# Where a helper's instructions stand in the queues: attention behind the last MLP tile, weight conversion behind the last but one

## The chip, the cores and the metric

One core of a Trainium2 chip runs the whole program. The metric is device microseconds from the first to the last instruction plus what lies around them, as measured by the runs. TensorE (PE), VectorE (DVE), ScalarE (ACT), GpSimd (POOL) and SyncE (SP, which here only issues transfers) each work off their own queue in order.

## What is computed

```python
scores  = scale * x @ state.T ;  a  = softmax(scores)  ; xread = a @ state      # 8 batches, 8 heads, x 512x64
scores2 = scale * state @ x.T ;  a2 = softmax(scores2) ; sread = a2 @ x         # state 32x64
rows = concat(xread, sread)          # per batch 512 + 32 rows, 512 wide
out  = relu(rows @ w_in)**2 @ w_out  # w_in 512x2048, w_out 2048x512
```

Inputs and output are float32; the weights arrive in a 64-bit form. The products are taken at nearly full float32 precision.

## The kernel before

**Precision by splitting.** `split` cuts a tile into a rounded part `hi` (a cast on ACT, L97) and the rest `lo` (a subtraction on DVE or POOL, L98). A product is then three matmuls: hi*hi, lo*hi, hi*lo.

**Weights.** Each of the 16 blocks of `w_in` (`w_raw`) and of `w_out` (`wo_raw`) comes as pairs of 32-bit words, 512 KB a block, into one of four `raw` buffers. `singles` makes float32 of them: one ACT instruction (L108) and three DVE instructions (L109, L113, L117). Then `w_in` (`wf`) is written back to DRAM (`wd`), and `w_out` is split into `wo_hi` and `wo_lo` (the latter on POOL) and stays.

**z.** Instead of xread @ w_in, the kernel computes z = state @ w_in per head once for four batches (`z_part`: matmuls `pz`, copies `z_stage` on ACT, to DRAM as `zd`), and later, per batch and 256 columns, reads it back (`z_fetch`: `z_raw`, split into `z_hi`, `z_lo`). With a = the softmax weights, a @ z is then the hidden layer.

**Attention.** Per batch there are two groups of four heads. Each loads x transposed (`xt_raw`), splits it (`xt_hl`, one buffer; from batch 2 on), multiplies by the state (`pq`, from batch 2 on; `pst` for batches 0 and 1), and runs the softmax: `st_low` (ACT), `st` (DVE), transpose `q1` (L303), maxima `nm2`, `m1`, subtraction (L316, on POOL for batches under 3), exp (L317), sums `s1`, multiplication (L325, on POOL for batches under 3), transpose back `at` (L327), split into `a_hi` (ACT) and `a_lo` (POOL). The `read` steps (`pt`, `e_hl`, `pr`, `both`, `sr`) make sread for the final MLP.

**The MLP.** `mlp` runs what is called a unit here: for 128 of the 2048 hidden columns of one batch, `up` makes 6 matmuls into `ph` (L392, from `a_hi`, `a_lo`, `z_hi`, `z_lo`), then relu `r` (ACT, L394), the square (ACT, L396, for the first ten units; DVE, L398, after), `g_hi` (ACT) and `g_lo` (DVE); `down` makes 12 matmuls into `po` (L418) two units later. A batch has 16 units. The first four stretches interleave batches 0 and 1: units 1 to 6 are batch 0, 7 to 16 batch 1, 17 to 26 batch 0, 27 to 32 batch 1. Units 33 to 48 are batch 2, and so on to unit 128; then 16 units of half the width do the sread rows.

**What sets the order.** The Python code calls `aux` twice in each unit, and `aux` hands out steps of two lists by their due times: `weights` (convert, load, `wo_load`, z products) and `reads` (attention of batches 1 and on, and the read steps). A scheduler then places all instructions on the engines' queues, by the order of the code, but anything whose inputs are ready may overtake what is not ready. So a step that the code has between two units may land on its queue well ahead of the unit.

Of the kernel before, what the change touches and what calls it, by code (L numbers as in the profile page):

```python
# [18 lines left out]
def memory_attention_then_relu2_ffn(  # L19
# [74 lines left out]
            zd[G, k] = dr.tile([P, NG, HG, FW], F32, name=f"zd_{G}_{k}")  # L94

    def split(hi, lo, src, eng_lo):
        nc.scalar.copy(out=hi, in_=src)  # L97
        eng_lo.tensor_sub(out=lo, in0=src, in1=hi.bitcast(F32))  # L98

    def singles(out_f, words):  # L100

        low, high = words[..., 0], words[..., 1]
        bits = out_f.bitcast(I32)
        nc.scalar.activation(out_f, high.bitcast(F32), AF.Abs, scale=2.0**-112)  # L108
        nc.vector.tensor_scalar(  # L109
            out=bits, in0=bits, scalar1=3, scalar2=0x7FFFFFF8,  # L110
            op0=ALU.logical_shift_left, op1=ALU.bitwise_and,
        )
        nc.vector.scalar_tensor_tensor(  # L113
            out=bits, in0=high, scalar=-0x80000000, in1=bits,
            op0=ALU.bitwise_and, op1=ALU.bitwise_or,
        )
        nc.vector.scalar_tensor_tensor(  # L117
            out=bits, in0=low, scalar=29, in1=bits,
            op0=ALU.logical_shift_right, op1=ALU.bitwise_or,
        )  # L120


    def z_state(G):
        if G == 0:
            raw = sb.tile([P, H, GB * N], F32, name="st_f", tag="x_hl", bufs=1)
            st["raw"] = raw
        else:
            raw = sb.tile([P, H, GB * N], F32, name="st_raw", tag="raw", bufs=RAW)
        for j in range(2):
            nc.sync.dma_start(out=raw[j * D:(j + 1) * D].rearrange("d h m -> d (h m)"), in_=stT[G])  # L130
        hi = sb.tile([P, H, GB * N], F32R, name="stz_hi", bufs=1)
        lo = sb.tile([P, H, GB * N], F32R, name="stz_lo", bufs=1)
        if G:
            split(hi, lo, raw, nc.gpsimd)
        else:
            for i in range(2):
                own = slice(i * D, (i + 1) * D)
                other = slice((1 - i) * D, (2 - i) * D)
                for v in (hi, lo):
                    nc.gpsimd.memset(v[other, i::2, :].bitcast(F32), 0.0)  # L140
                split(hi[own, i::2, :], lo[own, i::2, :], raw[own, i::2, :], nc.vector)
        st[G] = hi, lo

    def z_part(G, k, g):

        box = {}
        ccs = slice(g * NCC // NG, (g + 1) * NCC // NG)
        nq = NCC // NG

        def load():  # L150
            if G:
                box["wf"] = sb.tile([P, nq, FW], F32, name="wf", bufs=2)
                nc.sync.dma_start(out=box["wf"], in_=wd[k][:, ccs, :])
                return
            raw = sb.tile([P, nq, FW, 2], I32, name="w_raw", tag="raw", bufs=RAW)
            nc.sync.dma_start(out=raw.rearrange("p c f w -> p (c f w)"), in_=w_in[k * NG + g])
            box["raw"] = raw

        def convert():
            wf = sb.tile([P, nq, FW], F32, name="wf", bufs=2)  # L160
            singles(wf, box["raw"])
            nc.sync.dma_start(out=wd[k][:, ccs, :], in_=wf)
            box["wf"] = wf

        plain = G == 0 and k * NG + g < PLAIN_Z

        bank = dict(pool=ps_o, tag="po") if G == 0 and k == 0 else dict(pool=ps_x, tag="px")

        def cut():
            if plain:  # L170
                return
            wf = box["wf"]
            w2 = [sb.tile([P, nq, FW], F32R, name=f"w2_{i}", bufs=2) for i in range(2)]
            box["w2"] = w2
            if G == 0:
                split(w2[0], w2[1], wf, nc.vector)
                return
            for i, w in enumerate(w2):
                own = slice(i * D, (i + 1) * D)
                other = slice((1 - i) * D, (2 - i) * D)  # L180
                nc.scalar.copy(out=w[own], in_=wf[own])  # L181
                nc.gpsimd.tensor_sub(out=w[other], in0=wf[own], in1=w[own].bitcast(F32))  # L182

        def product(i):
            def run():
                own = slice(i * D, (i + 1) * D)
                pz = bank["pool"].tile([P, nq, FW], F32, name="pz", tag=bank["tag"])
                for q in range(nq):
                    h = g * HG + 2 * q + i
                    if plain:  # L190
                        nc.tensor.matmul(
                            pz[:, q, :], lhsT=st["raw"][own, h, :], rhs=box["wf"][own, q, :],
                            start=True, stop=True,
                        )
                        continue
                    st_hi, st_lo = st[G]
                    u, v = (w[:, q, :] for w in box["w2"])
                    todo = ((st_lo, u), (st_hi, u), (st_hi, v))
                    if G:
                        w = box["w2"][i][:, q, :]  # L200
                        todo = (st_lo, w), (st_hi, w)
                    for j, (a, w) in enumerate(todo):
                        nc.tensor.matmul(  # L203
                            pz[:, q, :], lhsT=a[:, h, :], rhs=w,
                            start=j == 0, stop=j == len(todo) - 1,
                        )
# [8 lines left out]
                nc.scalar.copy(out=stage, in_=pz)
                dst = zd[G, k].rearrange("p g (q i) f -> p g q i f", i=2)[:, g, :, i, :]
                nc.scalar.dma_start(out=dst, in_=stage)
            return run

        return load, convert, cut, [product(i) for i in range(2)]  # L220

    def z_fetch(b, k):
        if k or b:
# [157 lines left out]
    def mlp(width, fcs, first, rows, aux):  # L381
# [6 lines left out]
        def up(fc):  # L388
            ph = ps_h.tile([P, S], F32, name="ph", tag="ph")[:, :width]
            todo = first(fc)  # L390
            for i, (w, v) in enumerate(todo):
                nc.tensor.matmul(ph, lhsT=w, rhs=v, start=i == 0, stop=i == len(todo) - 1)  # L392
            r = sb.tile([P, S], F32, name="r", bufs=2)[:, :width]
            nc.scalar.activation(r, ph, AF.Relu)  # L394
            if units[0] < 10:
                nc.scalar.activation(ph, r, AF.Square)  # L396
            else:
                nc.vector.tensor_mul(out=ph, in0=ph, in1=r)  # L398
            units[0] += 1
            hi = sb.tile([P, S], F32R, name="g_hi", bufs=2)[:, :width]  # L400
            lo = sb.tile([P, S], F32R, name="g_lo", bufs=2)[:, :width]
            split(hi, lo, ph, nc.vector)
            gs[fc] = hi, lo

        def down(i):
# [35 lines left out]
    def wo_load(fc):  # L441
        k, i = divmod(fc, FPC)
        raw = sb.tile([P, DM, 2], I32, name="wo_raw", tag="raw", bufs=RAW)
        nc.sync.dma_start(
            out=raw.rearrange("p e w -> p (e w)"), in_=w_out[fc * P:(fc + 1) * P, :]
        )
        wf = sb.tile([P, DM], F32, name="wof", bufs=2)
        singles(wf, raw)
        if i == 0:
            wo[k] = [const.tile([P, FPC, DM], F32R, name=f"{n}{k}") for n in ("wo_hi", "wo_lo")]  # L450
        split(wo[k][0][:, i, :], wo[k][1][:, i, :], wf, nc.gpsimd)
# [23 lines left out]
    class Ahead:  # L475

        def __init__(self):
            self.steps, self.due, self.done = [], [], 0  # L480

        def add(self, steps, due, begin=0):
            self.steps += [(begin, s_) for s_ in steps]
# [23 lines left out]
    for b in range(B):
        for g in range(NG):
# [169 lines left out]
```

## Time and profile before

| what | value |
|---|---|
| median of 3 runs (lowest to highest) | 708.6 us (707.11 to 710.06) |
| the profiled execution: its own time | 708.43 us |
| its span, first to last instruction | 706.6 us |
| busy: PE, PE weight load, DVE, ACT, POOL | 669.8, 551.6, 452.2, 398.3, 199.3 us |
| granted TensorE clock, mean | 0.973 |

The profiled execution lies 0.2 us under the median, and 1.8 us of its time lie outside the span. The page divides the span into 40 slices of 17.7 us; a digit is the busy share in tenths. In the rows of the timeline the first number is the start in us from the span's start, the second the time from the start of the first to the end of the last of the instructions in the row. Instructions of one engine may overlap a little, since the next begins before the one ahead has drained.

### The profile page before, as it was taken

What the parts mean: (1) busy time and instruction counts of PE and PEld (TensorE: products, weight loads), DVE (VectorE), ACT (ScalarE), POOL (GpSimd) and SP (SyncE); (2) the same over time, 40 slices, a digit from 0 to 9 for tenths busy, and PEclk for the clock granted to TensorE, in tenths of its full rate; (3) what the DMA queues carried; (4) which work ended last, traced back from release to release, by engine and by line L of the source; (5) the groups of instructions that cost most, each with busy time, mean ns of one, the idle gap of its engine ahead of it and who ended that gap; (6) DMA issues with size and microseconds to landing.
All of it is one profiled execution on the core that took longest, in us unless ns stands there. A gap on an engine that the chain in (4) does not pass through costs nothing.

```text
span 706.6 us, 9753 instructions
## 1 busy us (share of the span) xinstructions
PE 669.8 (95%) x3152; PEld 551.6 (78%) x3152; DVE 452.2 (64%) x757; ACT 398.3 (56%) x727; POOL 199.3 (28%) x181
## 2 busy tenths in 40 slices
PE   4688789999999999999999999999999999999997
PEld 2355668778888888888888878888888888888996
DVE  4859999758456944447945794797944445443553
ACT  3767687567565863467735653665654344332442
POOL 2314433345443540053403240344242022000000
PEclk8589999999999999999999999999999999999999
DMA  8898899435363542344423312412241112100421
GB/s 276 270 315 283 258 306 315 131 97 153 98 202 122 166 149 62 102 135 120 135 78 120 87 48 74 139 58 90 89 150 61 30 31 90 31 16 0 130 80 32
DMA packets 74548, 90.58 MB, mean 128 GB/s; under 512 B 7680, under 2 KB 57600, under 8 KB 74496
## 3 DMA queue, kind: packets, MB, share of 16 engines
q1 hardware_dynamic: 56896, 72.90, 32.9%
q10 hardware_dynamic: 17600, 17.04, 7.1%
q8 instruction: 25, 0.41, 0.3%
q14 instruction: 27, 0.22, 0.1%
HBM read 60.03 MB, written 29.88 MB: 127 GB/s over the span
## 4 chain that ended last, share of the span: by engine, by line
PE 79%; DVE 8%; DMA 6%; issue 2%; ACT 2%; SPq 1%; POOL 0%; DVEq 0%; ACTq 0%; POOLq 0%
PE po L418 47%; PE ph L392 25%; PE pz L203 3%; DMA wo_raw<-w_out 2%; PE pr L355 2%; DMA sp_raw<-stP 2%; PE pq L288 1%; PE pt L343 1%; DVE wf L117 1%; DVE wf L113 1%; DVE z_lo L98 1%; DVE g_lo L98 1%; DMA zd<-z_stage 1%; DMA xt_raw<-xT 1%; DVE wf L109 1%
## 5 line engine op out<-in xcount | busy, mean ns | idle before, releaser
L418 PE MATMUL po<-wo_hi,g_hi 128*128 128x512 f32 x544 | 217.3, 400 | 0.6 <-ACT g_hi L97 0.5
L418 PE MATMUL po<-wo_lo,g_hi 128*128 128x512 f32 x544 | 215.0, 395 | 0.0
L398 DVE TENSOR_TENSOR ph<-ph,r 128x512 f32<-128x512 f32 (+1 forms) x134 | 89.1, 665 | 169.1 <-ACT r L394 168.9
L394 ACT ACTIVATE r<-ph 128x512 f32<-128x512 f32 (+1 forms) x144 | 82.1, 572 | 171.0 <-PE ph L392 169.6
L418 PE MATMUL po<-wo_hi,g_lo 128*128 128x512 f32 x544 | 152.2, 392 | 0.0
L418 PEld LDWEIGHTS po<-wo_hi,g_hi 128*128 128x128 f32 x544 | 103.9, 191 | 22.4 <-ACT g_hi L97 2.0
L418 PEld LDWEIGHTS po<-wo_lo,g_hi 128*128 128x128 f32 x544 | 103.9, 191 | 19.5
L418 PEld LDWEIGHTS po<-wo_hi,g_lo 128*128 128x128 f32 x544 | 101.5, 189 | 21.1 <-issue 1.0
L98 DVE TENSOR_TENSOR g_lo<-ph,g_hi 128x512 fp32r<-128x512 f32 (+1 forms) x144 | 94.4, 656 | 36.3 <-ACT g_hi L97 27.7
L97 ACT CAST g_hi<-ph 128x512 fp32r<-128x512 f32 (+1 forms) x144 | 81.0, 563 | 57.9 <-DVE ph L398 51.7
L392 PE MATMUL ph<-a_hi,z_hi 128*128 128x512 f32 x256 | 81.4, 399 | 2.6 <-DVE nm L306 1.5
L392 PE MATMUL ph<-a_lo,z_hi 128*128 128x512 f32 x256 | 80.1, 392 | 0.0
L392 PE MATMUL ph<-a_hi,z_lo 128*128 128x512 f32 x256 | 80.0, 394 | 0.0
L98 POOL TENSOR_TENSOR xn_hl<-xn_raw,xn_hl 128x1024 fp32r<-128x1024 f32 x16 | 38.9, 2432 | 138.0 <-ACT xn_hl L97 71.2
L182 POOL TENSOR_TENSOR w<-wf,w 64x512 fp32r<-64x512 f32 x32 | 43.0, 1343 | 74.9 <-ACT w L181 69.8
L392 PEld LDWEIGHTS ph<-a_hi,z_hi 128*128 128x128 f32 x256 | 47.6, 190 | 15.2 <-DVE g_lo L98 2.1
L392 PEld LDWEIGHTS ph<-a_hi,z_lo 128*128 128x128 f32 x256 | 48.5, 190 | 10.4
L392 PEld LDWEIGHTS ph<-a_lo,z_hi 128*128 128x128 f32 x256 | 48.2, 189 | 10.5 <-issue 0.3
L98 POOL TENSOR_TENSOR xt_hl<-xt_raw,xt_hl 128x1024 fp32r<-128x1024 f32 x12 | 28.9, 2406 | 75.4 <-ACT xt_hl L97 43.7
L98 DVE TENSOR_TENSOR z_lo<-z_raw,z_hi 128x512 fp32r<-128x512 f32 x64 | 47.9, 750 | 0.3 <-DMA wd<-wf 0.3
L97 ACT CAST z_hi<-z_raw 128x512 fp32r<-128x512 f32 x64 | 39.2, 615 | 1.3 <-DMA wd<-wf 0.8
L98 POOL TENSOR_TENSOR wo_lo<-wof,wo_hi 128x512 fp32r<-128x512 f32 x16 | 25.2, 1578 | 51.4 <-ACT wo_hi L97 51.4
(97 smaller groups left out, 833.7 us busy)
## 6 DMA issues: line engine op xcount, KB each, us to landing
zd<-z_stage ACTq DMA_DIRECT2D x64, 256.0 KB, 3.2
z_raw<-zd SPq DMA_DIRECT2D x252, 64.0 KB, 2.4
xt_raw<-xT SPq DMA_DIRECT2D x16, 512.0 KB, 3.8
w_raw<-w_in SPq DMA_DIRECT2D x16, 512.0 KB, 5.3
wo_raw<-w_out SPq DMA_DIRECT2D x16, 512.0 KB, 5.8
xn_raw<-xn SPq DMA_DIRECT2D x16, 512.0 KB, 3.9
out<-sum SPq DMA_DIRECT2D x32, 256.0 KB, 2.5
wd<-wf SPq DMA_DIRECT2D x16, 256.0 KB, 3.7
```

The costliest lines, as they stand in the source:

```text
L97: nc.scalar.copy(out=hi, in_=src)
L98: eng_lo.tensor_sub(out=lo, in0=src, in1=hi.bitcast(F32))
L109: nc.vector.tensor_scalar(out=bits, in0=bits, scalar1=3, scalar2=0x7FFFFFF8, op0=ALU.logical_shift_left, op1=ALU.bitwise_and,)
L113: nc.vector.scalar_tensor_tensor(out=bits, in0=high, scalar=-0x80000000, in1=bits, op0=ALU.bitwise_and, op1=ALU.bitwise_or,)
L117: nc.vector.scalar_tensor_tensor(out=bits, in0=low, scalar=29, in1=bits, op0=ALU.logical_shift_right, op1=ALU.bitwise_or,)
L182: nc.gpsimd.tensor_sub(out=w[other], in0=wf[own], in1=w[own].bitcast(F32))
L203: nc.tensor.matmul(pz[:, q, :], lhsT=a[:, h, :], rhs=w, start=j == 0, stop=j == len(todo) - 1,)
L355: nc.tensor.matmul(pr[:, q].rearrange("p i c -> p (i c)"), lhsT=my["e"][:, t, q].rearrange("p i n -> p (i n)"), rhs=my["xn"][:, t, q].rear ...
L392: nc.tensor.matmul(ph, lhsT=w, rhs=v, start=i == 0, stop=i == len(todo) - 1)
L394: nc.scalar.activation(r, ph, AF.Relu)
L398: nc.vector.tensor_mul(out=ph, in0=ph, in1=r)
L418: nc.tensor.matmul(po[t], lhsT=g, rhs=w, start=i == 0 and j == 0, stop=i == last and j == 2)
```

## The change

Two lists of "last instructions" are kept, by engine. `marks` holds the newest of: each unit's `g_hi` cast (ACT) and `g_lo` subtraction (DVE), and each load of `w_raw` or `wo_raw` (SP). `earlier` holds, for ACT and DVE, what `marks` held before the newest unit. While a step of `reads` is traced, each of its instructions on ACT, DVE and SP must come behind `marks` on its queue; while a step of `weights` is traced, its instructions on ACT and DVE must come behind `earlier`. These are orders within one queue; no wait on a semaphore is added. PE and POOL have no marks. The loading of the first state tile and its splitting into `stz_hi` and `stz_lo`, one step before, are two steps now (`z_state_load`, `z_state_cut`): the splitting is written behind the first conversions and products, and its DVE subtractions must come behind the last conversion instruction of block 1 of `w_in` on DVE's queue.

```diff
 def split(hi, lo, src, eng_lo):
+    a = nc.scalar.copy(out=hi, in_=src)
+    return a, eng_lo.tensor_sub(out=lo, in0=src, in1=hi.bitcast(F32))
+def mark(*those):
+    for i in those:
+        marks[i.ins.engine] = i.ins
+def behind(those):
+    stack = ExitStack()
+    for i in those.values():
+        stack.enter_context(tc.issue_after(i))
+    return stack
...
-            split(hi, lo, ph, nc.vector)
+            those = split(hi, lo, ph, nc.vector)
+            earlier.update({i.ins.engine: marks[i.ins.engine] for i in those if i.ins.engine in marks})
+            mark(*those)
...
         def next(self):
-            emit(self.steps[self.done][1])
+            with behind(self.behind):
+                emit(self.steps[self.done][1])
...
-        q["cut_t"], q["scores"], q["soft1"], p["soft1b"], q["soft1b"], lambda: z_state(0),
+        q["cut_t"], q["scores"], q["soft1"], p["soft1b"], q["soft1b"], lambda: z_state_load(0),
...
+    with tc.issue_after(z0[1][4]["done"].ins):
+        z_state_cut(0)
-    weights, reads = Ahead(), Ahead()
+    weights, reads = Ahead(earlier), Ahead(marks)
```

The loads in `z_part.load` and `wo_load` are wrapped in `mark(...)`. The changed file is 30 lines longer, so its rows carry other line numbers: L303, L305, L306, L315 of before are L327, L329, L330, L339 there, L322 to L325 are L346 to L349, L327 is L351, L398 is L422, L599 is L629, L156, L162 and L444 are L180, L186 and L470.

**The first loads, SP's queue.** Before, from the second pair of `w_in` blocks on (`sp_raw`, `xt_raw` are loads for the attention, `wd` the writing back of a converted block):

```order
L156 DMA w_raw_229<-w_in 128x1024
L245 DMA sp_raw_306<-stP 128x128
L245 DMA sp_raw_1688<-stP 128x128
L264 DMA xt_raw_310<-xT 128x2x512
L264 DMA xt_raw_386<-xT 128x2x512
L162 DMA wd_0_83<-wf_182 128x512
L156 DMA w_raw_255<-w_in 128x1024
L245 DMA sp_raw_2226<-stP 128x128
L245 DMA sp_raw_3079<-stP 128x128
L162 DMA wd_0_83<-wf_188 128x512
L444 DMA wo_raw_257<-w_out 128x1024
```

The same place after the change:

```order
L180 DMA w_raw_219<-w_in 128x1024
L186 DMA wd_0_83<-wf_172 128x512
L180 DMA w_raw_255<-w_in 128x1024
L186 DMA wd_0_83<-wf_178 128x512
L470 DMA wo_raw_257<-w_out 128x1024
L186 DMA wd_1_84<-wf_249 128x512
L180 DMA w_raw_274<-w_in 128x1024
L470 DMA wo_raw_276<-w_out 128x1024
L186 DMA wd_1_84<-wf_268 128x512
L180 DMA w_raw_291<-w_in 128x1024
L186 DMA wd_2_85<-wf_285 128x512
L470 DMA wo_raw_293<-w_out 128x1024
```

The six loads of the attention of later batches are gone from here; `sp_raw_306` and `xt_raw_310` (batch 1) follow the last row shown, the others much later.

**Batch 1's first unit (unit 7), DVE's queue.** `g_lo_752` is the low part of unit 7, `at_679` the last transpose of batch 1's attention. Before, the ten rows that end with `g_lo_752`, which is row 138 of the queue (`at_679` is row 118, so twenty rows up):

```order
L109 TENSOR_SCALAR wof_757<-wof_757 128x512
L117 SCALAR_TENSOR_TENSOR wf_884<-w_raw_701,wf_884 128x512
L113 SCALAR_TENSOR_TENSOR wof_757<-wo_raw_755,wof_757 128x512
L117 SCALAR_TENSOR_TENSOR wof_757<-wo_raw_755,wof_757 128x512
L98 TENSOR_TENSOR z_lo_946<-z_raw_940,z_hi_945 128x512
L98 TENSOR_TENSOR w2_1_985<-wf_884,w2_0_984 128x512
L109 TENSOR_SCALAR wf_1002<-wf_1002 128x512
L113 SCALAR_TENSOR_TENSOR wf_1002<-w_raw_810,wf_1002 128x512
L117 SCALAR_TENSOR_TENSOR wf_1002<-w_raw_810,wf_1002 128x512
L98 TENSOR_TENSOR g_lo_752<-ph_732,g_hi_751 128x512
```

After, with `g_lo_752` as row 113 and `at_679` as row 110:

```order
L125 TENSOR_SCALAR wof_757<-wof_757 128x512
L98 TENSOR_TENSOR w2_1_787<-wf_695,w2_0_786 128x512
L129 SCALAR_TENSOR_TENSOR wof_757<-wo_raw_755,wof_757 128x512
L351 STREAM_TRANSPOSE at_679<-q1_563 128x512
L133 SCALAR_TENSOR_TENSOR wof_757<-wo_raw_755,wof_757 128x512
L98 TENSOR_TENSOR z_lo_946<-z_raw_940,z_hi_945 128x512
L98 TENSOR_TENSOR g_lo_752<-ph_732,g_hi_751 128x512
L125 TENSOR_SCALAR wf_804<-wf_804 128x512
```

The conversions of `wf_804`, `wf_884` and `wf_1002` now stand behind unit 7, and unit 7 is 25 rows nearer to the start.

**Batch 2's first unit (unit 33), DVE's queue.** `pq_1809` and `pq_1815` are the score products of batch 2's second group, `q1_1821` its softmax, `at_1857` and `at_1896` the last transposes of the two groups. Before, this stands around unit 21 (`g_lo_1429`):

```order
L294 TENSOR_TENSOR st_1808<-pq_1809,st_low_1812 64x512
L294 TENSOR_TENSOR st_1808<-pq_1815,st_low_1818 64x512
L327 STREAM_TRANSPOSE at_1857<-q1_1751 128x512
L303 STREAM_TRANSPOSE q1_1821<-st_1808 128x512
L305 TENSOR_REDUCE nm2_1823<-st_1808 128x1
L98 TENSOR_TENSOR sp_hl_77<-sp_raw_2226,sp_hl_77 64x4x32
L98 TENSOR_TENSOR g_lo_1429<-ph_1409,g_hi_1428 128x512
```

After, it stands between unit 32 and unit 33, whose square is the last row (`sum_1238` gathers the last `po` tiles of batch 1):

```order
L629 TENSOR_TENSOR sum_1238<-sum_1238,po0_1759 128x512
L629 TENSOR_TENSOR sum_1238<-sum_1238,po1_1760 128x512
L339 TENSOR_REDUCE m1_1873<-q1_1821 128x16
L629 TENSOR_TENSOR sum_1238<-sum_1238,po2_1761 128x512
L629 TENSOR_TENSOR sum_1238<-sum_1238,po3_1762 128x512
L330 TENSOR_SCALAR nm2_1823<-nm2_1823 128x1
L351 STREAM_TRANSPOSE at_1857<-q1_1751 128x512
L346 TENSOR_REDUCE s1_1891<-q1_1821 128x16
L347 TENSOR_SCALAR s1_1891<-s1_1891 128x16
L348 RECIPROCAL s1_1891<-s1_1891 128x16
L351 STREAM_TRANSPOSE at_1896<-q1_1821 128x512
L422 TENSOR_TENSOR ph_1944<-ph_1944,r_1960 128x512
```

The two subtractions `st_1808`, the transpose `q1_1821` and the first maxima (`nm2_1823`) are the four rows ahead of the fence (rows 230 to 233), so the second group's whole softmax now stands between the units 32 and 33.

The same place on ACT's queue after the change (`g_hi_1887` is unit 32, `r_1960` unit 33, `w2` a cast of a weight block for the z products):

```order
L97 CAST g_hi_1887<-ph_1877 128x512
L97 CAST stz_hi_1970<-st_raw_1967 128x1024
L205 CAST w2_0_1976<-wf_1974 64x512
L317 COPY st_low_1812<-pq_1809 64x512
L205 CAST w2_1_1977<-wf_1974 64x512
L317 COPY st_low_1818<-pq_1815 64x512
L341 ACTIVATE q1_1821<-q1_1821 128x512
L333 ACTIVATE e2_1826,s2_1827<-st_1808,nm2_1823 128x512
L97 CAST a_hi_1686<-at_1857 128x512
L97 CAST a_hi_1686<-at_1896 128x512
L418 ACTIVATE r_1960<-ph_1944 128x512
```

POOL's queue at the same place after the change:

```order
L98 TENSOR_TENSOR stz_lo_1971<-st_raw_1967,stz_hi_1970 128x1024
L206 TENSOR_TENSOR w2_0_1976<-wf_1974,w2_0_1976 64x512
L349 TENSOR_TENSOR q1_1751<-q1_1751,s1_1852 128x512
L206 TENSOR_TENSOR w2_1_1977<-wf_1974,w2_1_1977 64x512
L340 TENSOR_TENSOR q1_1821<-q1_1821,m1_1873 128x512
L98 TENSOR_TENSOR a_lo_1687<-at_1857,a_hi_1686 128x512
L349 TENSOR_TENSOR q1_1821<-q1_1821,s1_1891 128x512
L98 TENSOR_TENSOR a_lo_1687<-at_1896,a_hi_1686 128x512
```

All of the second group's softmax from `st_low_1812` on is behind unit 32 on ACT, and on POOL the splitting of the second state tile, two weight casts' low parts and the first group's `a_lo` stand in front of its multiplication (the last but one row). On PE, the last `pq_1815` was row 442 and the first matmul of unit 33 (`ph_1944`) row 661 of the queue; now they are rows 608 and 641, with 24 `po` matmuls (units 31 and 32) and 8 `pz` matmuls between them, and the 12 `ph` matmuls of units 33 and 34 behind them, up to the first `po` of unit 33 (row 651). On ACT the last `z_stage` of the first four batches' eighth z block (`z_stage_1506`) is row 211 and the `z_hi_1576` that needs it, for unit 25, row 215; before, they were rows 205 and 229. Counted in units, the last `a_hi` cast of a batch stood 8 units ahead of the batch's first unit for batch 2, and 12, 6, 6, 10 and 18 for batches 3 to 7; now it is 1 unit for batch 2, 2 for 3 and 4, and 4 for 5 to 7. The steps are the same and no instruction is added or removed on the engines.

More of the change, by code (lines that the diff above doesn't have):

```diff
@@ L96, in split @@
     def split(hi, lo, src, eng_lo):
-        nc.scalar.copy(out=hi, in_=src)
-        eng_lo.tensor_sub(out=lo, in0=src, in1=hi.bitcast(F32))
+        a = nc.scalar.copy(out=hi, in_=src)
+        return a, eng_lo.tensor_sub(out=lo, in0=src, in1=hi.bitcast(F32))
+    marks = {}
+    earlier = {}
+    def mark(*those):
[6 more added lines that the diff above has]
+        return stack
     def singles(out_f, words):
@@ L116, in singles @@
         )
-        nc.vector.scalar_tensor_tensor(
+        return nc.vector.scalar_tensor_tensor(
             out=bits, in0=low, scalar=29, in1=bits,
@@ L123, in z_state, with z_state_load @@
     def z_state(G):
+        z_state_load(G)
+        z_state_cut(G)
+    def z_state_load(G):
         if G == 0:
@@ L130, in z_state, with z_state_cut @@
             nc.sync.dma_start(out=raw[j * D:(j + 1) * D].rearrange("d h m -> d (h m)"), in_=stT[G])
+        st["raw", G] = raw
+    def z_state_cut(G):
+        raw = st["raw", G]
         hi = sb.tile([P, H, GB * N], F32R, name="stz_hi", bufs=1)
@@ L155, in load @@
             raw = sb.tile([P, nq, FW, 2], I32, name="w_raw", tag="raw", bufs=RAW)
-            nc.sync.dma_start(out=raw.rearrange("p c f w -> p (c f w)"), in_=w_in[k * NG + g])
+            mark(nc.sync.dma_start(out=raw.rearrange("p c f w -> p (c f w)"), in_=w_in[k * NG + g]))
             box["raw"] = raw
@@ L160, in convert @@
             wf = sb.tile([P, nq, FW], F32, name="wf", bufs=2)
-            singles(wf, box["raw"])
+            box["done"] = singles(wf, box["raw"])
             nc.sync.dma_start(out=wd[k][:, ccs, :], in_=wf)
@@ L218, in product @@
             return run
-        return load, convert, cut, [product(i) for i in range(2)]
+        return load, convert, cut, [product(i) for i in range(2)], box
     def z_fetch(b, k):
@@ L443, in wo_load @@
         raw = sb.tile([P, DM, 2], I32, name="wo_raw", tag="raw", bufs=RAW)
-        nc.sync.dma_start(
+        mark(nc.sync.dma_start(
             out=raw.rearrange("p e w -> p (e w)"), in_=w_out[fc * P:(fc + 1) * P, :]
-        )
+        ))
         wf = sb.tile([P, DM], F32, name="wof", bufs=2)
@@ L475, in memory_attention_then_relu2_ffn, with __init__ @@
     class Ahead:
-        def __init__(self):
-            self.steps, self.due, self.done = [], [], 0
+        def __init__(self, behind):
+            self.steps, self.due, self.done, self.behind = [], [], 0, behind
         def add(self, steps, due, begin=0):
@@ L504, in memory_attention_then_relu2_ffn @@
     lags = {}
-    for _, _, c, ps in zs[0] + zs[1]:
+    for _, _, c, ps, _ in zs[0] + zs[1]:
         lags[ps[0]] = [(c, 2)]
```

## The prediction

> **What bounds the kernel now.** I read the slices of the page first, then the busy time of each engine by stage.
>
> ```profile
> PE   4688789999999999999999999999999999999997
> DVE  4859999758456944447945794797944445443553
> ```
>
> TensorE is full from the sixth or seventh slice on, with a dip in the last; VectorE is full in the slices four to seven only. By stage (columns: stage, its length, then busy time of PE, PEld, DVE, ACT and POOL, granted clock, DMA share, GB/s):
>
> ```profile
> 0.00:101.40 101.40, 71.78 (x269) 50.32 (x270) 80.04 (x138) 67.67 (x131) 35.60 (x34) 0.82 0.87 284
> 101.40:140.00 38.60, 38.03 (x179) 31.48 (x179) 34.45 (x51) 26.77 (x48) 12.27 (x9) 0.99 0.73 231
> 220.00:240.00 20.00, 19.72 (x96) 16.34 (x95) 19.48 (x35) 16.07 (x31) 10.30 (x6) 1.00 0.58 185
> 240.00:650.00 410.00, 409.50 (x1920) 341.06 (x1919) 245.87 (x405) 217.02 (x383) 105.28 (x103) 1.00 0.27 84
> ```
>
> In the first 101.4 us PE is idle for 29.6 us and its clock is 0.82; DVE is busy for 80.0. From there on PE never waits for more than a moment: 0.6 us idle in 38.6, 0.5 us in 410. So the end is set by two things: when the saturated stretch begins, and any hole that opens in it. A microsecond won on DVE, ACT or POOL behind 101.4 us is worth nothing; a microsecond of PE idleness put there costs one.
>
> The saturated stretch begins where the `down` of unit 7, batch 1's first, begins:
>
> ```profile
> 87.37 0.70 DVE L327 STREAM_TRANSPOSE at<-q 128x512 f32<-128x512 f32 x1
> ...
> 101.39 0.63 PE L418 MATMUL po<-wo_hi,g_hi 128*128 128x512 f32 x1
> 101.87 0.68 DVE L98 TENSOR_TENSOR g_lo<-ph,g_hi 128x512 fp32r<-128x512 f32 x1
> ```
>
> The last transpose of batch 1's attention (`at`) is over at 88.07. Unit 7 could go on from there, but its `g_lo` starts at 101.87: between the two on DVE's queue stand twenty instructions, nearly all conversions of weights.
>
> **The change part by part.** No instruction is added or taken away, so only places move, and I cost three places.
>
> **1. The head: a gain, part of it taken back.** Up to `g_lo` of unit 7 DVE's queue held 138 rows, of which 80.04 us were busy, 0.58 a row; now `g_lo` is row 113. Twenty-five rows fewer are 25 x 0.58 = 14.5 us less, since DVE is what is full there. Two things take from it. First, the chain behind the last transpose was covered by twenty rows and now by two. For what it costs I need the mean times (fourth number; us of busy time ahead of it):
>
> ```profile
> L97 ACT CAST a_hi<-at 128x512 fp32r<-128x512 f32 x16 | 9.8, 620 | 10.4 <-DVE at L327 8.4 <-PE ph L392 1.9
> L98 POOL TENSOR_TENSOR a_lo<-at,a_hi 128x512 fp32r<-128x512 f32 x16 | 22.0, 1377 | 26.9 <-ACT a_hi L97 26.7
> L394 ACT ACTIVATE r<-ph 128x512 f32<-128x512 f32 x128 | 75.9, 595 | 145.4 <-PE ph L392 144.0 <-DMA z_raw<-zd 0.6 <-ACT z_stage L215 0.4
> L396 ACT ACTIVATE ph<-r 128x512 f32<-128x512 f32 x10 | 6.0, 612 | 0.1
> L97 ACT CAST g_hi<-ph 128x512 fp32r<-128x512 f32 x128 | 75.0, 587 | 56.9 <-DVE ph L398 50.7 <-PE po L418 2.7 <-PE ph L392 2.3
> ```
>
> `a_hi` 0.62, `a_lo` of both groups one after the other on POOL 2 x 1.38, the last `ph` matmuls some 0.45, `r` of units 7 and 8 2 x 0.60, the square and a cast between 2 x 0.61, `g_hi` 0.59: 6.9 us, where the three rows of DVE account for 3 x 0.58 = 1.7. So 5.2 us come back. Second, the loads of weights on SP are no longer in front of conversions by as much, because each needs one of the four `raw` buffers, and the conversion that frees it now stands behind units:
>
> ```profile
> wo_raw<-w_out SPq DMA_DIRECT2D x16, 512.0 KB, 5.8
> zd<-z_stage ACTq DMA_DIRECT2D x64, 256.0 KB, 3.2
> z_raw<-zd SPq DMA_DIRECT2D x252, 64.0 KB, 2.4
> ```
>
> A load that is issued only when a buffer comes free lands 5.8 us later, and what stands behind its conversion on ACT and DVE (the cast and the `g_lo` of the next unit) waits with it. The bounds are nothing (it lands behind other work) and 5.8, one landing in the open; I take 2.5, nearer to the middle, as the six attention loads that stood in front of the weights are gone from SP's queue. That makes 14.5 - 5.2 - 2.5 = 6.8: unit 7's `down` would start near 94.6 instead of 101.4. Of this 4.3 are not won, since 48 instead of 84 `pz` matmuls of the z products are done by then, and the other 36 run later, in saturated PE time:
>
> ```profile
> 233.81 0.28 PE L203 MATMUL pz<-w,stz_lo 128*128 128x256 f32 x1
> ...
> 234.77 0.40 PE L418 MATMUL po<-wo_hi,g_hi 128*128 128x512 f32 x1
> ...
> 236.38 0.39 PE L418 MATMUL po<-wo_lo,g_hi 128*128 128x512 f32 x1
> ```
>
> Eight `pz` go from 233.81 to 234.77, 0.12 each; the `po` from 234.77 to 236.38 are seven steps of 0.23. 36 x 0.12 = 4.3. **The head: -2.5.** Its ends are -10 (14.5 less the 4.3, both covers found elsewhere) and +3 (a landing of 5.8 in the open).
>
> **2. A hole at unit 33, batch 2's first: a loss.** Before, the last score products of batch 2 (`pq`) were 219 rows of PE's queue ahead of unit 33. Now PE has between them and the first `po` of unit 33 just 24 `po`, 8 `pz` and the 12 `ph` of units 33 and 34: 36 x 0.227 + 8 x 0.12 = 9.1 us. In that time the second group's softmax must run, which changes engines at every step:
>
> ```profile
> L97 ACT CAST stz_hi<-st_raw 128x1024 fp32r<-128x1024 f32 x1 | 1.1, 1057 | 0.0
> L181 ACT CAST w<-wf 64x512 fp32r<-64x512 f32 x32 | 19.8, 619 | 0.5
> L293 ACT COPY st_low<-pq 64x512 f32<-64x512 f32 x24 | 13.7, 583 | 7.0 <-PE pq L288 6.8
> L294 DVE TENSOR_TENSOR st<-pq,st_low 64x512 f32<-64x512 f32 x24 | 16.4, 682 | 3.1 <-ACT st_low L293 2.8
> L303 DVE STREAM_TRANSPOSE q<-st 128x512 f32<-128x512 f32 x12 | 8.4, 699 | 0.2
> L305 DVE TENSOR_REDUCE nm<-st 128x1 f32<-128x512 f32 x12 | 7.7, 643 | 0.0
> L599 DVE TENSOR_TENSOR sum<-sum,po 128x512 f32<-128x512 f32 x8 | 5.2, 679 | 0.0
> L315 DVE TENSOR_REDUCE m<-q 128x16 f32<-128x512 f32 x16 | 10.8, 676 | 0.1
> L316 POOL TENSOR_TENSOR q<-q,m 128x512 f32<-128x512 f32 x6 | 6.6, 1097 | 17.6 <-DVE m L315 10.3 <-DVE nm L306 7.3
> L317 ACT ACTIVATE q<-q 128x512 f32<-128x512 f32 x16 | 10.1, 628 | 0.7 <-DVE q L316 0.7
> L309 ACT ACTIVATE e<-st,nm 128x512 f32<-128x512 f32 x12 | 8.7, 726 | 1.6 <-DVE nm L306 1.4
> L182 POOL TENSOR_TENSOR w<-wf,w 64x512 fp32r<-64x512 f32 x32 | 43.0, 1343 | 74.9 <-ACT w L181 69.8 <-issue 4.1
> L98 POOL TENSOR_TENSOR stz_lo<-st_raw,stz_hi 128x1024 fp32r<-128x1024 f32 x1 | 2.4, 2399 | 0.2 <-ACT stz_hi L97 0.2
> L325 POOL TENSOR_TENSOR q<-q,s 128x512 f32<-128x512 f32 x6 | 6.8, 1135 | 10.2 <-DVE s L324 7.8 <-DVE s L339 2.2
> L327 DVE STREAM_TRANSPOSE at<-q 128x512 f32<-128x512 f32 x16 | 11.3, 706 | 2.8 <-POOL q L325 2.5
> ```
>
> With nothing else on the queues: `st_low` 0.58, `st` 0.68, transpose 0.70, maxima 0.68, subtraction 1.10, exp 0.63, sums some 0.68 like the maxima, multiplication 1.14, transpose back 0.70, `a_hi` 0.62, `a_lo` 1.38, `ph` 0.45, `r` 0.60, the square on DVE some 0.70, `g_hi` 0.59: 11.2. Less the 9.1 of cover that leaves a hole of 2.1 at least.
>
> With the queues as they now stand it is longer. From the last `pq`: `g_hi` of unit 32 is done after some 1.0, then on ACT `stz_hi` 1.06, `w` 0.62, `st_low` 0.58, `w` 0.62, `st_low` 0.58 (4.5). On DVE `st` 0.68, transpose 0.70, `nm` 0.64, two sums 1.36, maxima 0.68 (8.5). POOL is free by then: after `stz_hi` (2.1) it does `stz_lo` 2.40, two `w` 2 x 1.34 and the first group's multiplication 1.14 (8.3). The subtraction 1.10, the exp 0.63 (10.2). On ACT stands next the exp `e` 0.73 and the first group's `a_hi` 0.62 (11.5), and POOL takes that group's `a_lo`, 1.38, ahead of the multiplication 1.14 (14.0). Transpose 0.70, `a_hi` 0.62, `a_lo` 1.38 (16.7), then `ph`, `r`, square, `g_hi` 2.34 (19.1). That is 10.0 over the cover. I take one off, since an instruction starts a little before the one ahead has drained (0.08 us or so, some twelve times): 9.
>
> A hole of this kind leaves the clock low behind it, as one of 2.38 us in the head shows (number in brackets: idle time ahead):
>
> ```profile
> 59.53 0.39 PE L203 MATMUL pz<-w,stz_lo 128*128 128x256 f32 x1 [2.38 <-ACT e L309]
> ...
> 61.05 0.63 PE L418 MATMUL po<-wo_lo,g_hi 128*128 128x512 f32 x1
> ...
> 62.76 0.63 PE L418 MATMUL po<-wo_lo,g_hi 128*128 128x512 f32 x1
> ...
> 66.47 0.27 PE L203 MATMUL pz<-w,stz_lo 128*128 128x256 f32 x1
> ```
>
> From 61.05 to 62.76 four `po` take 0.43 each instead of 0.23, and the quick pace is back at 66.47. Of 5.4 slow us nearly half, 2 to 2.5, is lost; I take 2. The Trainium skill, "TensorE: Matmul & The Clock Gate", section "Part 1: The HAM clock gate", has the clock halved only after an idle window of about 3.4 us, and back after as long a busy one. This trace does not bear out the first half: 2.38 us idle were enough. By the page one slow window would cost an estimated 1.7 us, and the sum would be 0.3 lower.
>
> **The hole: +11.** Its ends are +2 (the bare chain, no slow clock) and +13 (no overlap, both slow terms).
>
> **3. z products just in time: +0.5.** The last `z_stage` of the first four batches' eighth z block stands four ACT rows ahead of the `z_hi` that reads it back for unit 25. Out and back take 3.2 + 2.4 us by the rows above, and the PE work ahead of unit 25's `ph` is some 18 x 0.23 = 4.1 per unit, two units. The ends are 0 and 3.
>
> Batches 3 to 7 keep 2 to 4 units, 8 to 16 us, between `a_hi` and first use: the same bare chain, 11.2 from the scores, is begun earlier there, so I cost nothing. POOL and PE are not marked, and the final part, where the reads' products are needed, has its last read steps three units later, still ahead of it.
>
> The sum, against the profiled execution's own 708.4 (0.2 under the median of 708.6): 708.4 - 2.5 + 11 + 0.5 = **717.4**.
>
> **The rivals.** *The head wins (faster).* If DVE's row count alone decides, the head gives -10; it needs the raw buffers to be free in time and the chain behind `at` to overlap with what is left. For it speaks 80.04 of 101.4 us busy on DVE. With the hole near its least, 2 to 3, that gives 708.4 - 10 + 2.5 = 701. It decides from the point at which the hole is smaller than the gain, so it also needs the softmax of batch 2 to run nearly without queueing, against which speak the two `w` casts and the `a_lo` that stand in front. Chance 0.15.
>
> *They cancel.* Head -7, hole +8: 708.4 + 1 = 709.4. This is what comes out if a few of the rows in front of the softmax are worked off earlier than I have them. Chance 0.18.
>
> *The conversions come too late as well.* If the weight loads wait in the open in the head (+3) and the hole is 13, it is 724. For it speaks that SP's loads now stand behind one another, each at 5.8 to landing, against it that 87% DMA share in the head falls as the attention's loads leave. Chance 0.1.
>
> **How the numbers follow.** Mine has 0.57, the sum being within some 5 us of 717.4 (712 to 722). The 80% range leaves the lower half of the first rival out and the upper end of the third: 704 to 724. A measurement of this kernel tells about 0.5%, 3.5 us, from no change: under 705.1 lies the first rival, 0.15; between that and 712.1 the second, 0.18; above it my forecast and the third rival, 0.67.
>
> **What would show it.** In the changed profile: (1) the PE row of unit 7's first `po` near 94 to 96, with the stretch behind it as full as before; at 101 the head has given nothing, at 90 the first rival is right. (2) An idle time of PE of 9 us in all between the last `pq` of batch 2 and unit 33's first `po`, released by `a_lo`, `r` or `g_hi`, and a few matmuls at 0.43 behind it; DVE and ACT with the softmax's rows in that hole. (3) A wait below 1 us ahead of unit 25. I am wrong if batch 2's `pq` come much earlier than their place in the queue suggests, if the hole is under 4 us, or if other batches' first units show holes too.

## Result and the profile after

| | before | after |
|---|---|---|
| median (lowest to highest), run side by side | 709.2 us (707.1 to 710.1) | 729.7 us (726.4 to 732.2) |
| ratio, 95% interval | | 1.029 (1.024 to 1.034) |
| profiled execution, span | 706.6 us | 727.2 us |
| busy PE, DVE | 669.8, 452.2 us | 676.3, 448.6 us |

The kernel became slower by 20.5 us, where 9 were forecast and 724 was the upper end. The slices of the changed kernel's page (18.2 us each) show the two places:

```profile
PE   4588859999996999999999999999999999999997
DVE  4846866764474647745585576567655876644453
```

PE's sixth slice is a 5 and its thirteenth a 6; before, they were 8 and 9. DVE, full from the fourth to the seventh slice before, is at 6 or 8 there. By stage, with the columns as in the prediction:

```profile
0.00:106.60 106.60, 70.03 (x233) 46.54 (x233) 69.13 (x114) 59.65 (x115) 31.53 (x33) 0.79 0.72 231
106.60:220.00 113.40, 113.15 (x524) 94.63 (x525) 72.07 (x119) 63.98 (x116) 16.98 (x11) 0.98 0.48 156
220.00:240.00 20.00, 12.01 (x42) 8.58 (x41) 10.32 (x19) 7.39 (x15) 10.16 (x9) 0.74 0.26 87
240.00:650.00 410.00, 409.07 (x1949) 343.32 (x1949) 263.44 (x444) 238.44 (x422) 138.73 (x130) 1.00 0.33 103
```

Behind 106.6 us PE is as full as before (0.25 us idle in 113, 0.9 in 410), save between 220 and 240 us, where it was busy for 19.7 of 20 before and is now for 12.0, at a clock of 0.74.

**The hole at unit 33** is where the prediction put it. PE's timeline, from the `pz` between the units 32 and 33 on, with the idle time ahead and its releaser in brackets:

```profile
223.24 0.28 PE L227 MATMUL pz<-w,stz_hi 128*128 128x256 f32 x1
224.91 0.39 PE L227 MATMUL pz<-w,stz_lo 128*128 128x256 f32 x1 [1.40 <-POOL w L206]
...
227.92 1.22 PE L416 MATMUL ph<-a_hi,z_hi 128*128 128x512 f32 x2 [2.26 <-ACT a_hi L97]
231.67 0.79 PE L416 MATMUL ph<-a_hi,z_hi 128*128 128x512 f32 x1 [2.53 <-ACT a_hi L97]
...
233.54 0.63 PE L416 MATMUL ph<-a_hi,z_hi 128*128 128x512 f32 x1
233.97 1.05 PE L416 MATMUL ph<-a_hi,z_lo 128*128 128x512 f32 x2
...
238.10 0.50 PE L444 MATMUL po<-wo_hi,g_hi 128*128 128x512 f32 x1 [1.80 <-ACT g_hi L97]
238.44 0.40 PE L444 MATMUL po<-wo_lo,g_hi 128*128 128x512 f32 x1
238.68 0.39 PE L444 MATMUL po<-wo_hi,g_hi 128*128 128x512 f32 x1
```

The four waits are 8.0 us, for POOL's `w`, for the two `a_hi` and for unit 33's `g_hi`. The `ph` in between go at 0.43 (233.54 to 233.97) instead of 0.23; for the 12 of them that is 12 x 0.20 = 2.4 us more. From 238.44 on the pace is quick again. So the hole is 10.4 us, of 11 forecast.

**The head** went the other way. Unit 7's `down`, which was to start near 94.6, starts at 106.55:

```profile
93.60 0.70 DVE L351 STREAM_TRANSPOSE at<-q 128x512 f32<-128x512 f32 x1
...
97.75 0.70 DVE L351 STREAM_TRANSPOSE at<-q 128x512 f32<-128x512 f32 x1
98.38 0.64 DVE L133 SCALAR_TENSOR_TENSOR wof<-wo_raw,wof 128x512 int32<-128x512 int32 x1
105.00 0.69 DVE L98 TENSOR_TENSOR z_lo<-z_raw,z_hi 128x512 fp32r<-128x512 f32 x1 [5.98 <-ACT z_hi L97]
...
106.55 0.79 PE L444 MATMUL po<-wo_hi,g_hi 128*128 128x512 f32 x1 [2.98 <-ACT g_hi L97]
```

The last transpose of batch 1's attention now begins at 97.75, where it began at 87.37. From its end to unit 7's first `po` it is 106.55 - 98.45 = 8.1 us, against 101.39 - 88.07 = 13.3 before: the twenty rows in between are gone and 5.2 us with them, but the transpose itself is 10.4 later, and 10.4 - 5.2 is the 5.2 us that unit 7 is late. DVE did have less to do up to unit 7, 69.13 us instead of 80.04; but it was idle for 37.5 of 106.6 us, before for 21.4 of 101.4. Those 16.1 us of new idle time outweigh the 10.9 of work. What DVE, ACT and SP wait for where loads and conversions meet, in the first 98.9 us (us in total, times, longest), before:

```profile
DVE wf L109 <- ACT wf L108: 9.3, 1, 9.3
DVE wof L109 <- ACT wof L108: 6.2, 2, 4.1
ACT wof L108 <- DMA wo_raw<-w_out: 4.1, 2, 3.0
SPq L444 <- DVE wof L117: 3.3, 2, 1.9
```

and after:

```profile
DVE wf L125 <- ACT wf L124: 14.8, 5, 9.2
DVE wof L125 <- ACT wof L124: 8.7, 6, 2.9
DVE g_lo L98 <- ACT g_hi L97: 3.4, 3, 1.5
DVE z_lo L98 <- ACT z_hi L97: 3.0, 1, 3.0
ACT wof L124 <- DMA wo_raw<-w_out: 8.2, 6, 2.7
SPq L470 <- DVE wof L133: 21.2, 4, 5.7
```

DVE waits for ACT's first conversion step, ACT for the load of `wo_raw`, and SP, which issues that load, for the last conversion step on DVE (L133), which frees a raw buffer. The three wait for each other in a ring; SP's part of it went from 3.3 to 21.2 us. Of DVE's new idle time up to unit 7 the waits for ACT's conversion step are 23.5 - 15.5 = 8.0 us, a half. The largest other one is the 5.98 in the `z_lo` row above: there DVE waits for the chain behind the last transpose, which twenty rows covered before.

Besides, fewer `pz` were done when unit 7's first `po` began, 96 instead of 132 (stage, its length, busy time of PE, PEld and ACT on `pz`, clock, DMA share, GB/s; before, then after):

```profile
0.00:101.39 101.39, 27.27 (x132) 20.31 (x132) 17.34 (x33) 0.82 0.86 284
0.00:106.55 106.55, 21.72 (x96) 15.04 (x96) 13.20 (x26) 0.79 0.72 231
```

So 36 x 0.12 = 4.3 us of work are put off into the full stretch, and the head costs 5.2 + 4.3 = 9.5 us. The eight `po` that follow go at 0.43, as the `ph` ahead of the wait of 2.98 us did, and take 3.5 us, up to 110.08; before, they took 2.1, up to 103.52. With these 1.4 us, the hole's 10.4 and 0.9 us less of small waits elsewhere in PE's full stretch (2.1 before, 1.2 after) it is 20.4 of the 20.6 us between the two spans.

### The profile page after: what moved, and what is told of

Its sections match the earlier page's. It is cut to its first block, busy times and chain, and to the rows that moved or that the text cites. A ratio compares the mean times of both kernels' runs of the same rounds, so it can differ in the third digit from the quotient of the medians.

```text
span 727.2 us, 9743 instructions
## 1 busy us (share of the span) xinstructions
PE 676.3 (93%) x3152; PEld 555.7 (76%) x3152; DVE 448.6 (62%) x757; ACT 398.1 (55%) x727; POOL 197.4 (27%) x181
## 4 chain that ended last, share of the span: by engine, by line
PE 81%; DMA 6%; ACT 4%; DVE 4%; issue 2%; POOL 1%; SPq 1%; ACTq 0%; DVEq 0%; POOLq 0%
PE po L444 47%; PE ph L416 26%; PE pz L227 3%; DMA wo_raw<-w_out 3%; PE pr L379 2%; DMA z_raw<-zd 2%; PE pq L312 1%; DMA w_raw<-w_in 1%; PE pt L367 1%; DMA st_raw<-stT 1%; DVE wf L133 1%; ACT wof L124 1%; ACT r L418 1%; ACT g_hi L97 0%; ACT z_hi L97 0%
## 5 line engine op out<-in xcount | busy, mean ns | idle before, releaser
L444 PE MATMUL po<-wo_hi,g_hi 128*128 128x512 f32 x544 | 216.8, 398 | 12.2 <-ACT g_hi L97 12.1
L444 PE MATMUL po<-wo_lo,g_hi 128*128 128x512 f32 x544 | 214.7, 395 | 0.0
L422 DVE TENSOR_TENSOR ph<-ph,r 128x512 f32<-128x512 f32 (+1 forms) x134 | 88.9, 664 | 140.7 <-ACT r L418 140.2
L444 PE MATMUL po<-wo_hi,g_lo 128*128 128x512 f32 x544 | 153.3, 391 | 0.0
L444 PEld LDWEIGHTS po<-wo_hi,g_hi 128*128 128x128 f32 x544 | 103.8, 191 | 36.2 <-ACT g_hi L97 15.2
L444 PEld LDWEIGHTS po<-wo_lo,g_hi 128*128 128x128 f32 x544 | 103.9, 191 | 20.8
L444 PEld LDWEIGHTS po<-wo_hi,g_lo 128*128 128x128 f32 x544 | 100.7, 188 | 19.8 <-DVE wof L133 0.3
L416 PE MATMUL ph<-a_hi,z_hi 128*128 128x512 f32 x256 | 83.4, 406 | 14.5 <-ACT a_hi L97 11.5
L416 PE MATMUL ph<-a_lo,z_hi 128*128 128x512 f32 x256 | 83.0, 401 | 0.0
L416 PE MATMUL ph<-a_hi,z_lo 128*128 128x512 f32 x256 | 83.0, 405 | 0.0
L416 PEld LDWEIGHTS ph<-a_lo,z_hi 128*128 128x128 f32 x256 | 50.1, 196 | 11.0
L416 PEld LDWEIGHTS ph<-a_hi,z_lo 128*128 128x128 f32 x256 | 50.2, 196 | 10.9
L98 DVE TENSOR_TENSOR z_lo<-z_raw,z_hi 128x512 fp32r<-128x512 f32 x64 | 49.4, 771 | 10.8 <-ACT z_hi L97 10.8
L98 POOL TENSOR_TENSOR wo_lo<-wof,wo_hi 128x512 fp32r<-128x512 f32 x16 | 22.2, 1385 | 99.1 <-ACT wo_hi L97 99.1
L239 ACT COPY z_stage<-pz 128x512 f32<-128x512 f32 x64 | 37.2, 587 | 11.6 <-PE pz L227 11.2
```

The source lines that it names most:

```text
L98: return a, eng_lo.tensor_sub(out=lo, in0=src, in1=hi.bitcast(F32))
L444: nc.tensor.matmul(po[t], lhsT=g, rhs=w, start=i == 0 and j == 0, stop=i == last and j == 2)
```

## Experiments

Twelve kernels were run, each against the kernel before on the same chip. That kernel's own median beside them lay between 707.2 and 709.4 us, so where a few us matter the ratios are compared. Beside the time stands the start of unit 7's `g_hi` on ACT, 98.9 us before and 105.9 after, as a measure of the head. "Marks" are the orders that the change adds.

| run | marks kept on | us, median | ratio to before (95%) | unit 7's `g_hi` |
|---|---|---|---|---|
| change | conversions, attention of all batches | 729.7 | 1.024 to 1.034 | 105.9 |
| e1 | conversions | 717.6 | 1.009 to 1.017 | 105.6 |
| e2 | attention of all batches | 721.0 | 1.015 to 1.026 | 102.8 |
| e3 | as the change, batch 2 free | 717.8 | 1.011 to 1.018 | 106.5 |
| e4 | as the change, batch 1 free | 723.2 | 1.017 to 1.028 | 97.5 |
| e5 | as the change, 5 raw buffers | 745.1 (one run) | | 102.0 |
| e6 | as the change, 3 raw buffers | 737.5 (one run) | | 110.8 |
| e7 | as the change, batches 1 and 2 free | 709.3 | 1.000 to 1.003 | 94.4 |
| e8 | attention of batches 3 on, reads | 702.5 | 0.988 to 0.995 | 94.7 |
| e9 | none | 710.4 | 1.001 to 1.004 | 102.8 |
| e10 | as the change, none on SP | 729.7 | 1.026 to 1.032 | 104.4 |
| e11 | as the change, batch 2 handed out earlier | 716.5 | 1.007 to 1.013 | 104.8 |
| e12 | as e8, state tile split as before | 703.3 | 0.989 to 0.995 | 95.3 |

**e1, e2: one list at a time.**

```diff
-    weights, reads = Ahead(earlier), Ahead(marks)
+    weights, reads = Ahead(earlier), Ahead({})     # e1
+    weights, reads = Ahead({}), Ahead(marks)       # e2
```

> Only the conversions of weights are kept behind the last but one unit; the attention steps carry no marks. Two places are in question, the head (unit 7's first po, 106.55 us in the changed kernel against 101.39 before, and fewer z products done by then) and the hole at unit 33. Theory A, the marks on the conversions make the head late: the hole is gone, the head stays, unit 7 at 105 to 107, time 716 to 720. Theory B, the marks on batch 1's attention make the head late: unit 7 at 101 or earlier, time 705 to 710.

> Only the attention steps are kept behind the last unit; the conversions carry no marks. Theory A (conversions make the head late): unit 7 back near 101, the hole stays, time 718 to 722. Theory B (attention makes it late): unit 7 at 105 to 107 and the hole, time 727 to 731.

e1 has no hole, and unit 7 is as late as in the change: theory A's figures. By the sum used above its head costs 9.1 us (first `po` of unit 7 at 106.20, 4.8 later than before, with 96 `pz` done), and its profiled span is 9.9 longer than before (716.5). e2 has the hole (its window from 215 to 245 has PE busy for 22.2 of 30 us) and unit 7 at 102.8, near A's figure too, but 3.9 us later than before. Its first `po` is 2.1 us later (103.49), but 144 `pz` are done by then instead of 132, which is 1.4 us of work, so the head loses next to nothing. So marks on conversions alone are enough to make the head late, and marks on attention alone are not. Unit 7 stands at 102.8 in e9 too, which has no marks at all, so its place in e2 does not speak for the marks.

**e3: batch 2's attention without marks.**

```diff
-            with behind(self.behind):
-                emit(self.steps[self.done][1])
+            step = self.steps[self.done][1]
+            with behind({} if step in free else self.behind):   # free: order(2)
+                emit(step)
```

> As the changed kernel, but the attention steps of batch 2 carry no marks; its last score products then stand 73 rows ahead of unit 33 on PE, where they are 33 in the changed kernel. If the hole at unit 33 costs its 9 us of idle time and some 2 of slow clock: PE idle under 3 us there, time 718 to 722. Rival, the hole is only moved to the next place where this work is wanted: 726 to 730.

The time fell by 11.8 us to 717.8 (by the ratios, 1.0291 and 1.0145, it is 10.3), and the window of the hole is full, at full clock:

```profile
220.00:240.00 20.00, 20.00 (x98) 16.80 (x97) 12.43 (x23) 13.64 (x24) 14.34 (x9) 1.00 0.65 204
```

The head stayed where it was (106.5). The hole's price is shown, and nothing of it came back elsewhere.

**e4: batch 1's attention without marks** (the same edit with `order(1)`).

> As the changed kernel, but the attention steps of batch 1 carry no marks, so that only later batches and the conversions do. Theory B (batch 1's attention, kept behind the units of batch 0, makes the head late): unit 7 at 98 to 102, time 719 to 725. Theory A (conversions): unit 7 stays at 105 to 107, time 727 to 731.

Unit 7's `g_hi` is at 97.5, ahead of before and a little ahead of theory B's 98 to 102, and the time is 6.5 us below the change, in B's range, in the presence of the marks on conversions. By the ratios it is 4.9 us, and their intervals overlap, so the gain in time is less sure than the 8.4 us by which unit 7 comes earlier. So A and B are both true, and neither alone: the head is late when conversions are held back and the attention of batch 1 as well. With e1 that leaves a question, since there batch 1 is free and unit 7 late; e7 answers it.

**e5, e6: the ring.** One raw buffer more, and one fewer.

```diff
-    RAW = 4
+    RAW = 5      # e5, with LATE = 2 in place of 3 to make room
+    RAW = 3      # e6
```

> As the changed kernel with five instead of four raw buffers for the loads of weights; to make room for it the read steps come two batches behind instead of three (LATE 2), which leaves DVE's queue up to unit 7 as it was but loads unit 33 and what follows, so only the head is read: the start of the 3rd and the 7th g_hi on ACT (66.4 and 105.9 us in the changed kernel, 59.4 and 98.9 before). Theory R, loads wait for a raw buffer and conversions wait for loads, a ring of latencies: the 7th g_hi at 98 to 103, and DVE's waits for the conversions' ACT step (23.5 us in the changed kernel) fall by a third or more. Theory O, the place of the conversions behind the units alone delays them: 104 to 107.

> As the changed kernel with three instead of four raw buffers. Theory R (ring of raw buffers): each load is issued a conversion later, the 7th g_hi at 112 or later and time 736 or more. Theory O (place in the queues alone): 7th g_hi at 105 to 108, time 728 to 732.

Unit 7's `g_hi`, in e5 and in e6:

```profile
102.03 0.60 ACT L97 CAST g_hi<-ph 128x512 fp32r<-128x512 f32 x1
```

```profile
110.76 0.59 ACT L97 CAST g_hi<-ph 128x512 fp32r<-128x512 f32 x1
```

With three, four and five buffers it is 110.8, 105.9 and 102.0: four to five us a buffer. e5 came out in the range of theory R; DVE's waits for the conversions fell by 30%, 23.5 to 16.5 us, where a third was named, and ACT's wait for `wo_raw` rose, from 8.2 to 10.4. In the first 98.9 us SP's own waits for DVE's last step on `w_out` ahead of its loads of `w_raw` and `wo_raw` fell from 24.1 to 8.7 us; with three buffers they were 21.3, no longer than with four. e6 fell 1.2 us short of R's 112, but its time, 737.5, was in R's range, and ACT's wait for that load doubled:

```profile
ACT wof L124 <- DMA wo_raw<-w_out: 17.4, 6, 4.8
```

Each is a single run, and the order of some instructions changed with the number of buffers. The three starts of unit 7 speak for the ring as a part of the head; the kernel before was not run with another number of buffers, so it is not shown how much of these 4 to 5 us the marks bring. e5's time says nothing of the ring, since its read steps come a batch earlier and unit 33's hole was wider for it (PE busy for 18.1 of 30 us from 215 on).

**e7, e8: both repairs, and then the conversions free as well.**

```diff
+    for b in (1, 2):
+        free.extend(order(b))
-    weights, reads = Ahead(earlier), Ahead(marks)
+    weights, reads = Ahead({}), Ahead(marks)        # e8 only
```

> As the changed kernel, but the attention of batches 1 and 2 carries no marks; marks on later batches and on the conversions stay. If the two effects found so far are separate (batch 1 free gave -6.5, batch 2 free -11.8), they add: 729.7 - 18.3 = 711 (709 to 714), unit 7 at 97 to 99 and no hole at unit 33. Rival, batch 2's attention that runs ahead takes the head's gain back, as the kernel with marks on the conversions alone suggests (7th g_hi at 105.6): 716 to 719.

> Marks on the attention of batches 3 and on alone; conversions, batch 1 and batch 2 carry none. If the marks on conversions are what makes the rest of the head late: unit 7 at 96 to 101 with some 120 z products done, no hole, time 702 to 708, faster than or like before. Rival, what keeps later batches' work away from the head is worth nothing because the conversions bound it: 707 to 712.

e7 is a little better than the sum of e3 and e4: 729.65 - 11.83 - 6.50 = 711.3, measured 709.3 (by the ratios 1.0076 and 1.0016). Unit 7 is at 94.4, earlier than the 97 to 99 expected. Against e1, where it is at 105.6, e7 differs only in that the steps of batches 3 and on, with the read steps that come in the same list, stay marked. So in e1 it was these that ran ahead into the head. e8, which holds back nothing else, is faster than the kernel before, by 0.5 to 1.2%. Unit 7's first `po` starts at about the same time in both (95.33, in e7 95.08), but with 120 `pz` done where e7 has 96: 24 x 0.12 = 2.9 of the 3.6 us between the two profiled spans, 704.6 and 701.0. The medians are 6.8 us apart.

**e9, e12: the later split of the state tile.** e9 is the change without marks on either list; e12 is e8 with `z_state(0)` in its old place.

> Neither list carries marks: of the change only the split of the first state tile behind the first conversions is left. If that step is neutral, the time is that of the kernel before, 705 to 711, and the gain of the kernel with marks on batches 3 and on alone (702.5) comes from those marks. Rival: the later splitting gives that gain by itself, 700 to 704, unit 7 at 94 to 97.

> The kernel before with marks on the attention of batches 3 and on alone (no marks on conversions or on batches 1 and 2, the first state tile split where it was). If the gain of 0.9% seen with the later split comes from keeping later batches away from the head and not from the split, this is 700 to 705, faster than before by 0.5 to 1.2%. Rival: the gain needs both, and this is 706 to 710.

The split by itself gains nothing (0.1 to 0.4% slower, and unit 7's `g_hi` 3.9 us later than before; what makes it later was not tried; by the sum above its head costs 4.4 us, with the first `po` at 104.39 and 120 `pz`, and its profiled span is 3.2 longer), and the gain of e8 stays without it: 0.992 (0.989 to 0.995). In e12's DVE queue the rows that have left the part ahead of unit 7's `g_lo` are the eight `s` (L338, L339) and four `e` (L340) rows of the read steps and two conversions. By the groups of the trace of before the read rows are 3.7 us:

```profile
L340 DVE TENSOR_SCALAR e<-e,s 128x512 f32<-128x512 f32 x16 | 10.2, 638 | 0.1
L339 DVE RECIPROCAL s<-s 128x1 f32<-128x1 f32 x16 | 2.5, 155 | 0.2
L338 DVE TENSOR_SCALAR s<-s 128x1 f32<-128x1 f32 x16 | 2.3, 143 | 0.5 <-ACT e L309 0.4
```

4 x 0.638 + 4 x 0.155 + 4 x 0.143 = 3.7, and unit 7 comes 3.6 us earlier (95.3 for 98.9). That these rows alone make the difference was not tried: two loads for later batches (`sp_raw`) left the head of SP's queue too, and one of 512 KB for a read step (`xn_raw`, at 67.27 us before).

**e10: no marks on SP.** The two loads of weights are no longer passed to `mark`.

> As the changed kernel without marks on the loads of weights (SP); the marks on ACT and DVE stay, and DVE's order up to unit 7 is unchanged, but the attention loads of batch 1 stand ahead of the loads of weights as before. If batch 1's attention is late through its loads: 7th g_hi at 98 to 102, time 720 to 725. If it is late through its place on DVE and ACT: 104 to 107, time 727 to 731.

729.7, the time of the change, and unit 7 at 104.4: batch 1's attention is late through its place on DVE and ACT, not through its loads: these start at 5.8 and 8.6 us again, where in the change they start between 34.6 and 51.9.

**e11: batch 2's steps handed out six units earlier, under all the marks.**

```diff
-            reads.add(steps, 2 * begins[b] - 1, 2 * ends[b - 2] if b > 1 else 0)
+            ahead = 12 if b == 2 else 0
+            reads.add(steps, 2 * begins[b] - 1 - ahead, 2 * ends[b - 2] - ahead if b > 1 else 0)
```

> As the changed kernel with all its marks, but the steps of batch 2's attention are handed out six units earlier (begin and due time both 12 calls earlier). If the hole at unit 33 is only a matter of how many units lie between the last step and the first use: PE idle under 2 us there, time 717 to 721, like the kernel with batch 2 free (717.8). Rival: the steps then delay the units 21 to 26 they stand among (the marks put them behind each unit on DVE and ACT), and a hole of 3 us or more opens there: 722 to 728.

716.5, a little better than e3 and than the 717 to 721 expected, and no hole opens among the units that the steps now stand between:

```profile
190.00:215.00 25.00, 24.96 (x110) 19.99 (x109) 19.79 (x35) 12.54 (x24) 5.71 (x5) 1.00 0.28 94
215.00:240.00 25.00, 25.00 (x120) 20.95 (x119) 14.71 (x26) 16.69 (x29) 14.34 (x9) 1.00 0.53 169
```

The marks as such cost nothing there; what costs is a list of due times that was made for steps that could still run ahead.

## Why the prediction was right or wrong

**The bound: right.** PE is full behind unit 7 in both kernels, and the end is set by when that begins and by the hole.

**The hole: right, in place, mechanism and size.** 9 us idle and 2 of slow clock forecast; 8.0 and 2.4 measured, and 10.3 to 11.8 when it is closed. PE's first wait, 1.40 for POOL's `w`, was not seen; it lies within the hole that the sum took as a whole. The gaps were 1.4 to 2.5 us here, and the `ph` behind those of 2.26 and 2.53 went at 0.43. As in the head, the idle window of about 3.4 us of the Trainium skill ("TensorE: Matmul & The Clock Gate", section "Part 1: The HAM clock gate") does not describe what this trace shows.

**The head: wrong in sign, -2.5 forecast and +9.5 measured, with 1.4 us of slow clock behind it.** The step that failed is "Twenty-five rows fewer are 25 x 0.58 = 14.5 us less, since DVE is what is full there". It took DVE's rows away and held its idle time constant. The work did fall, by 10.9 us, and the exposed chain behind the last transpose came out near the estimate (8.1 us from the transpose's end, 6.9 forecast for its steps; 6.0 us of it are DVE's wait). But DVE's idle time grew by 16.1 us, and 8.0 of them are waits for conversions. The term that should have held these was "one landing in the open; I take 2.5". As the wait rows show it, a conversion behind a unit delays the freeing of its raw buffer, the next load, and the next conversion, which again stands behind a unit, so the wait came back with every turn. DVE alone waited 6 times for `wof`, and unit 7 moves by 4 to 5 us a buffer (e5, e6, one run each). The second omission was batch 1's own attention. Its rows were counted as fewer ahead of the last transpose, so it was taken to end earlier; held behind the units of batch 0 on DVE and ACT, it ended 10.4 us later. e4 gives 5 to 6.5 us of the 20.5 back by freeing it alone, with unit 7 8.4 us earlier.

**z products put off: right,** 36 forecast and 36 measured, 4.3 us. **z just in time:** +0.5 forecast; PE's only wait between 107 and 223 us is one of 0.25. **Batches 3 to 7:** no term, and there is only one wait of 0.93 us, far behind, like the 0.50 before.

**The rivals.** The third one, conversions too late as well (+3 in the head, 724), was the right mechanism with a chance of 0.1; its price of one landing made it too small, and with it the range. Its +3 does not follow from the terms either: 14.5 - 5.2 - 5.8 - 4.3 is a loss of 0.8. The argument held against it, that the DMA share would fall as loads leave, was true (0.87 to 0.72 up to unit 7) and beside the point: the loads were waited for because they were issued late. The transfers themselves were no slower: `wo_raw` took 5.0 us from issue to landing in the median, 5.8 before. The first rival's gain in the head exists, but only in part and without the marks on conversions and on batches 1 and 2: e8 and e12.

## What to carry to other kernels

An order that holds work back needs a due time with room for that work's whole latency: here batch 2's steps had been handed out late because they could overtake, and moving the due time by six units repaired 13 us with every mark in place. Where a load, its conversion and the freeing of its buffer form a ring, holding the conversion back can be paid once per turn of the ring, so count turns and buffers, not only rows of the busiest queue. Hold back only what is not wanted soon: marking batches 3 and on with the read steps gained 0.8 to 0.9%, while the change, which marks what is needed next as well, cost 2.9%.

## What the runs showed of the hardware

The clock again fell after short gaps: in the hole the `ph` behind waits of 2.26 and 2.53 us went at 0.43 us, and the stage's granted clock is 0.74. The wait of 1.40 ahead of them was followed by `pz` at the quick pace (0.12 from 225.14 on), and behind the one of 1.80 the pace of 0.23 is back at 238.44. A hole split into four waits of at most 2.5 us thus cost nearly a third on top of its idle time (2.4 on 8.0 us).
